# The second weight's blocks begin to be converted in the first stage, and a table of order offsets is set anew

## The chip, the cores and the metric

The kernel runs on one core of one Trainium2 chip. The metric is the device time of one execution in microseconds (us); of the kernel before it is the median of three runs.

## The reference, cut to what matters

Attention over 4 batches and 8 heads with a bias that depends on the two positions, and then a feed-forward pair of matrix products with a gate between them. q, k and v are float32. The two weights of the second half come as 64-bit floats.

```python
# attention: q, k, v are (4, 8, 576, 64)
scores = scale * np.matmul(q, k.transpose(0, 1, 3, 2))
...
x = (psi_rel / psi_i)[..., None]
h = np.maximum(x @ w1 + b1, 0.0)      # 32 hidden values for each pair of positions
scores = scores + (h @ w2).transpose(2, 0, 1)[None]
...
attn_out = softmax(scores) @ v
# second half: x (2304, 512), w_in (512, 2048), w_out (2048, 512)
h = x @ w_in
g = h * (1.0 / (1.0 + np.exp(-h)))
return g @ w_out
```

## The kernel before

The 576 query rows of a head are cut into chunks c = 0 to 3 of 128 rows and c = 4 of 64 rows. The heads go in pairs hp = 0 to 3. The 2304 rows of the second half are five blocks (BLOCKS): two of 384 rows and three of 512.

The program has three stretches. **First**, batches 0 and 1 are done chunk by chunk (ORDER: c = 4, then 0 to 3), and beside them `bias_tile` makes the bias: 36 tiles of 16 rows, each of four relus over a table (kind bias_f, DVE or ACT), a product (bias_mm, PE), an eviction from PSUM in two instructions (bias_ev), a store to DRAM, from which the chunks load it again. **Second**, batches 2 and 3 are done, interleaved with the first two blocks of the second half (`ff_block`). **Third** come the last three blocks (`ff_super`), which trade products for sums.

A chunk (`chunk`) is: scores on PE (s_quad, s_row or s_mm); one DVE pass that adds the bias and takes the maximum (max); exp on ACT; transposes on PE (t_mm); their eviction (p_ev). `visit` ends with the product with v (pv) and stores the result to DRAM (x_d).

`prepare` brings in one block of a weight. `narrow` loads it as 64-bit words (kind ld_wide, 512 KB) into a buffer of pool G and makes float32 of it: one instruction on ACT (abs), four on DVE (clamp, shift, low, sign). `split` then splits it into two halves in another G buffer: split_hi on ACT, split_lo on GpSimd (POOL) or DVE. There are 16 blocks of each weight. A block of w_out stays in its G buffer to the end; G has 27 buffers.

What stands where is set by no loop. Each operation is recorded with the engines that may run it, a duration and a due time; a list scheduler in Python (`Plan.order`) then gives out the operations by due time as engines, buffers and banks come free in its own reckoning. Its answer fixes the instruction order of each engine and of SP, whose queue issues every DMA in that order; a DMA that waits for a buffer holds up those behind it. The due times come from T0, DC, B1, BD and the other constants, and each group of operations has its own offset from the table SHIFT:

```python
group = 4 * self.groups + (0 if "SP" in where else 1 if "PE" in where else 2)
prio += SHIFT.get(group, 0.0)
```

Where PE has nothing to run early on (until WU in the plan's time) the plan puts in `warm_up` products on zeros.

Of the kernel before, what the change touches and what calls it, by code (L numbers as in the profile page):

```python
# [24 lines left out]
FIRST, RAW, QUAD, ORDER = (0, 1), (0, 1), (0, 1, 2, 3), (4, 0, 1, 2, 3)  # L25
# [3 lines left out]
T0, DC, B1, BD, GAP0, DF, DS, WU = 26.19, (3.9, 3.82), 68.9, 4.82, -2.44, 5.0, 12.64, 24  # L29


PACE, LEAD, STEP = (1.32, 2.55), 24.62, (9.49, 8.69)


def f(ap):
# [333 lines left out]
def attention_moe_kernel(ctx: ExitStack, tc: tile.TileContext, q, k, k0, v, small, w_in, w_out, lut, ident_d, out):  # L369
# [668 lines left out]
    def ff_block(blk, t0, step):  # L1038
        xs = split_x(blk, t0 - 8)
        acc = [bank("acc", 1) for _ in range(3)]  # L1040
        for fi in range(NF):
            t = t0 + step * fi
            if blk == 0:
                wr = prepare(t - 5, w_in[fi])
                load("st_in", t - 1, [win_b[fi]], lambda e, wr=wr, fi=fi: SP.dma_start(out=win_d[fi], in_=f(tl(wr).rearrange("p a n -> p (a n)"))), 524288, reads=[wr])
                if wo[fi] is None:
                    wo[fi] = prepare(t - 2, w_out[128 * fi:128 * fi + 128, :])
# [14 lines left out]
    for c in ORDER:  # L1062
        for st in range(8 * c, min(8 * c + 8, 36)):
            bias_tile(st, (t - B1 if c != ORDER[0] else -60) + BD * (st - 8 * c))
        for hp in range(4):
# [3 lines left out]
            for b in FIRST if c == ORDER[-1] else ():  # L1069
                factors(b, hp, sq[b, hp], t)  # L1070
# [96 lines left out]
```

## Time and profile before

| | us |
|---|---|
| median of three runs | 704.21 |
| the runs | 704.07 to 705.24 |
| the profiled execution | 704.64 |
| its span, first to last instruction | 702.8 |
| PE busy in the span | 688.5 |
| VectorE (DVE) busy | 502.9 |
| ScalarE (ACT) busy | 402.1 |
| GpSimd (POOL) busy | 115.2 |

The profiled execution's own time is 1.84 us longer than its span and 0.43 us longer than the median. Busy time is added up over each engine's instructions; PE's records are pipelined, so a product that waits a little for its operands can still count as busy. The granted clock of PE was 0.999 of its higher level (2.4 GHz) over the span.

### The profile page before, as it was taken

How to read it: one execution, taken by the hardware profiler on the slowest of the kernel's cores; microseconds unless marked ns; L12 is line 12 of the kernel's file. 1: busy time of each engine (PE TensorE's matmuls, PEld its weight loads, DVE VectorE, ACT ScalarE, POOL GpSimd, SP SyncE). 2: the span in 40 equal slices, each digit the busy share in tenths (PEclk: the TensorE clock that was granted, in tenths of full speed). 3: DMA queues.
4: the chain of work that ended last, by engine and by line, in shares of the span. 5: the costliest groups of instructions: out<-in, count | busy, mean ns of one | idle time of the engine just before them, and what ended most of it. 6: DMA issues, size and time to landing. Idle time of an engine off the chain costs nothing.

```text
span 702.8 us, 14055 instructions
## 1 busy us (share of the span) xinstructions
PE 688.5 (98%) x5075; PEld 554.0 (79%) x5075; DVE 502.9 (72%) x1127; ACT 402.1 (57%) x882; POOL 115.2 (16%) x134
## 2 busy tenths in 40 slices
PE   9899999999999999999999999999999999999997
PEld 4356677777777777887778888998888888888896
DVE  7889767768988989998986788636374444844433
ACT  8889856667977787877755534423262222433222
POOL 1000000024623231411301111202030010311000
PEclk9999999999999999999999999999999999999999
DMA  8999577678788888658636979676475644795301
GB/s 247 311 325 301 165 258 217 199 219 277 247 248 283 291 257 304 190 204 280 255 127 190 356 270 346 231 271 215 156 237 201 217 157 153 269 280 207 154 1 60
DMA packets 75621, 161.26 MB, mean 229 GB/s; under 512 B 10656, under 2 KB 30752, under 8 KB 75552
## 3 DMA queue, kind: packets, MB, share of 16 engines
q1 hardware_dynamic: 75552, 160.37, 68.8%
q8 instruction: 40, 0.66, 0.4%
q14 instruction: 29, 0.24, 0.1%
HBM read 123.15 MB, written 37.18 MB: 228 GB/s over the span
## 4 chain that ended last, share of the span: by engine, by line
PE 76%; DVE 11%; DMA 5%; ACT 4%; issue 3%; POOL 0%; SPq 0%; DVEq 0%; ACTq 0%; POOLq 0%
PE psum L1001 18%; PE psum L944 15%; PE psum L662 8%; PE psum L785 8%; PE psum L864 7%; PE psum L841 7%; PE psum L753 5%; PE psum L490 3%; PE psum L762 3%; DVE G L769 3%; DMA xp<-x_d 2%; DVE pt L427 1%; DVE w L525 1%; ACT G L497 1%; DVE w L530 1%
## 5 line engine op out<-in xcount | busy, mean ns | idle before, releaser
L1001 PE MATMUL psum<-G 128*128 128x512 f32 x576 | 142.3, 392 | 0.9 <-DVE M L1015 0.5
L776 ACT ACTIVATE G<-G,sm 128x576 f32<-128x576 f32 (+1 forms) x144 | 111.3, 775 | 32.0 <-DVE sm L769 31.5
L1001 PEld LDWEIGHTS psum<-G 128*128 128x128 f32 x576 | 104.1, 188 | 20.2 <-DVE M L1015 1.0
L769 DVE CUSTOM_DVE_ANT_0 G<-psum,G 128x576 f32<-128x576 f32 (+1 forms) x144 | 105.4, 759 | 12.7 <-PE psum L762 5.6
L785 PEld LDWEIGHTS psum<-ident,G 128*128 128x128 f32 x656 | 72.5, 141 | 28.7 <-ACT G L776 12.3
L785 PE MATMUL psum<-ident,G 128*128 128x128 f32 x656 | 92.4, 278 | 2.7 <-DVE th L850 0.5
L662 PE MATMUL psum<-pt,M 128*64 128x128 f32 (+3 forms) x1120 | 85.7, 306 | 0.0
L955 DVE TENSOR_TENSOR M<-psum,M 128x256 f32<-128x256 f32 x72 | 30.2, 422 | 74.7 <-PE psum L944 56.5
L944 PE MATMUL psum<-pt,G 128*128 128x256 f32 x576 | 82.8, 286 | 0.3 <-DVE M L955 0.3
L944 PEld LDWEIGHTS psum<-pt,G 128*128 128x128 f32 x576 | 75.1, 190 | 6.8 <-DVE M L955 4.5
L662 PEld LDWEIGHTS psum<-pt,M 128*64 128x64 f32 x1120 | 61.3, 137 | 21.6 <-issue 4.6
L841 PE MATMUL psum<-M,G 128*128 128x384 f32 x384 | 77.5, 343 | 0.5 <-DVE M L430 0.5
L864 PE MATMUL psum<-G,M 128*128 128x512 f32 x288 | 74.4, 398 | 0.0
L425 ACT ACTIVATE pt<-psum 128x512 f32<-128x512 f32 (+3 forms) x104 | 53.4, 530 | 28.1 <-PE psum L785 20.3
L841 PEld LDWEIGHTS psum<-M,G 128*128 128x128 f32 x384 | 65.5, 188 | 5.0 <-issue 1.5
L982 ACT ACTIVATE M<-M 128x256 f32<-128x256 f32 (+1 forms) x48 | 24.7, 521 | 68.5 <-DVE M L955 67.7
L427 DVE COPY pt<-psum 128x640 f32<-128x640 f32 (+3 forms) x88 | 51.7, 607 | 13.0 <-PE psum L785 10.8
L864 PEld LDWEIGHTS psum<-G,M 128*128 128x128 f32 x288 | 52.0, 189 | 10.8 <-issue 1.8
L425 ACT ACTIVATE M<-psum 128x256 f32<-128x256 f32 x44 | 16.8, 382 | 72.2 <-PE psum L944 71.8
L762 PE MATMUL psum<-G,M 128*128 128x288 f32 x256 | 45.7, 307 | 0.6 <-DVE sm L769 0.6
L430 POOL TENSOR_TENSOR G<-M,G 128x512 fp32r<-128x512 f32 x12 | 15.7, 1313 | 179.7 <-ACT G L425 140.1
L762 PEld LDWEIGHTS psum<-G,M 128*128 128x128 f32 x256 | 37.3, 188 | 6.8 <-DVE sm L769 2.2
(90 smaller groups left out, 962.9 us busy)
## 6 DMA issues: line engine op xcount, KB each, us to landing
G<-ts_d SPq DMA_DIRECT2D x48, 512.0 KB
G<-win_d SPq DMA_DIRECT2D x40, 512.0 KB
G<-bias_d SPq DMA_DIRECT2D x32, 576.0 KB
bias_d<-G SPq DMA_DIRECT2D x36, 295.5 KB
G<-in_w_in_dram SPq DMA_DIRECT2D x16, 512.0 KB
G<-in_w_out_dram SPq DMA_DIRECT2D x16, 512.0 KB
win_d<-G SPq DMA_DIRECT2D x16, 512.0 KB
ts_d<-G SPq DMA_DIRECT2D x16, 512.0 KB
```

Source lines behind the costliest of these rows:

```text
L425: A.activation(out=out, in_=in_, func=AF.Copy)
L427: ENG[e].tensor_copy(out=out, in_=in_)
L662: T.matmul(out=tl(o)[x, d:d + n], lhsT=tl(vs)[:, (s + 1) % 5 * 128 + 64 * a:(s + 1) % 5 * 128 + 64 * a + 64], rhs=tl(pt)[:, s + 5 * a if s ...
L753: T.matmul(out=s[:, hf, 0:288], lhsT=tl(qst)[y, x0 + 128 * a:x0 + 128 * a + 128], rhs=tl(kst)[y, 416 * a:416 * a + 288], start=True, stop= ...
L762: T.matmul(out=s[:, hf, 0:288], lhsT=tl(qs)[:, x0 + 128 * a:x0 + 128 * a + 128], rhs=tl(part)[:, S * a + 288 * hf:S * a + 288 * hf + 288], ...
L769: V.tensor_tensor_reduce(out=mine(p, a).rearrange("p (a n) -> p a n", a=2), in0=tl(sps[a]).rearrange("p (a n) -> p a n", a=2)[:, :, 0:widt ...
L776: A.activation(out=mine(p, a), in_=mine(p, a), func=AF.Exp, scale=-1.0, bias=tl(sm)[:, i + a:i + a + 1], accum_out=tl(sq)[:, 2 * c + a:2 * ...
L785: T.transpose(out=tl(tp)[:, 128 * s:128 * s + 128], in_=tl(p)[:, 128 * (s0 + s):128 * (s0 + s) + 128], identity=ident)
L841: T.matmul(out=tl(hp)[:, 0:TB], lhsT=tl(wr)[:, x, 128 * cc:128 * cc + 128], rhs=tl(xs[cc])[:, y, :], start=(cc + m == 0), stop=(cc == NC - ...
L864: T.matmul(out=tl(acc[i]), lhsT=tl(gg)[:, x, 128 * i:128 * i + 128], rhs=tl(wo[fi])[:, y, :], start=(fi == 0 and m == 0), stop=(fi == NF - ...
L944: T.matmul(out=first(dst), lhsT=tl(w)[:, x, off + 128 * cc:off + 128 * cc + 128], rhs=tl(b)[:, at, y, :], start=(start and cc + i == 0), s ...
L1001: T.matmul(out=tl(acc[i]), lhsT=tl(gg)[:, x, 128 * i:128 * i + 128], rhs=tl(wo[fi])[:, y, :], start=(fi == 0 and j == 0), stop=(fi == NF - ...
```

## The change

A block of w_out is prepared with a due time that is earlier by WL * (1 - fi/16), with WL = 36: by 36 us of the plan's time for the first block and by 2.25 us for the last. The loop over the first stretch is written with PHASES in place of FIRST and ORDER; the phases name the same chunks and the same two batches in the same sequence, and GAP0 is now also added behind the last of them. The constants and all 1,100 or so offsets of SHIFT have new values. The scheduler, the operations, their shapes and their number are as before; only the number of warm-up products on PE differs (35 before, 47 after).

```diff
-FIRST, RAW, QUAD, ORDER = (0, 1), (0, 1), (0, 1, 2, 3), (4, 0, 1, 2, 3)
+RAW, QUAD, WL = (0, 1), (0, 1, 2, 3), 36.0
+PHASES = ((4, (0, 1)), (0, (0, 1)), (1, (0, 1)), (2, (0, 1)), (3, (0, 1)))
...
-T0, DC, B1, BD, GAP0, DF, DS, WU = 26.19, (3.9, 3.82), 68.9, 4.82, -2.44, 5.0, 12.64, 24
+T0, DC, B1, BD, GAP0, DF, DS, WU = 26.13, (3.57, 4.47), 63.81, 5.1, -2.44, 5.0, 11.17, 24
...
-PACE, LEAD, STEP = (1.32, 2.55), 24.62, (9.49, 8.69)
+PACE, LEAD, STEP = (1.32, 4.43), 24.66, (9.49, 9.87)
...
 SHIFT = {
-    0: 4.3, 1: 4.1, 2: 6.1, 4: -7.9, 5: 3.2, 6: 0.6, 8: 3.3, 9: -3.8, 10: -3.8, 12: -6.4, 13: -6.1, 14: -3.2,
...
                 if wo[fi] is None:
-                    wo[fi] = prepare(t - 2, w_out[128 * fi:128 * fi + 128, :])
+                    wo[fi] = prepare(t - 2 - WL * (1 - fi / NF), w_out[128 * fi:128 * fi + 128, :])
...
-    t = T0
-    for c in ORDER:
...
+    t, made, left = T0, set(), {b: 5 for _, some in PHASES for b in some}
+    for c, some in PHASES:
...
-        t += GAP0 if c != ORDER[-1] else 0
+        t += GAP0
```

In the rows that follow, the order before comes first and the order after second. Line numbers after are larger by 2.

**DVE at the start**, up to the first maximum (the custom instruction, shown as ISA, of line 769 before, 771 after). Line 484 (486) is a relu of the bias, line 499 (501) an eviction of a bias tile, which takes two rows.

```order
L499 TENSOR_SCALAR G<-psum,cb 128x31
L499 TENSOR_SCALAR G<-psum,cb 128x560
L484 TENSOR_SCALAR G<-lut_sb,cb 128x512 x3
L484 TENSOR_SCALAR G<-lut_sb,cb 128x496 x4
L484 TENSOR_SCALAR G<-lut_sb,cb 128x480 x2
L484 TENSOR_SCALAR G<-lut_sb,cb 128x448 x4
L484 TENSOR_SCALAR G<-lut_sb,cb 128x464
L769 ISA G,sm<-psum,G 128x640
L769 ISA sm 128x1
```

```order
L486 TENSOR_SCALAR G<-lut_sb,cb 128x448
L501 TENSOR_SCALAR G<-psum,cb 128x79
L501 TENSOR_SCALAR G<-psum,cb 128x512
L486 TENSOR_SCALAR G<-lut_sb,cb 128x480
L486 TENSOR_SCALAR G<-lut_sb,cb 128x448
L486 TENSOR_SCALAR G<-lut_sb,cb 128x480
L486 TENSOR_SCALAR G<-lut_sb,cb 128x432 x3
L486 TENSOR_SCALAR G<-lut_sb,cb 128x464
L501 TENSOR_SCALAR G<-psum,cb 128x111
L501 TENSOR_SCALAR G<-psum,cb 128x480
L771 ISA G,sm<-psum,G 128x640
L771 ISA sm 128x1
```

Two more evictions (of 79 and 512, and of 111 and 480 columns) stand ahead of the first maximum. Counted from the program's start, DVE runs 33 relus and 3 evictions ahead of it before, 34 and 5 after; ACT runs 18 relus and 7 evictions ahead of its first exp before, 22 and 7 after.

**SP's queue late in the first stretch**, where the first weight blocks are loaded (line 508 before, 510 after). in_k is a key of batch 2 or 3, bias_d the bias, in_q a query.

```order
L574 DMA G<-in_k_dram 128x1152
L633 DMA G<-bias_d_103 64x576
L602 DMA M<-in_q_dram 128x256
L508 DMA G<-in_w_in_dram 128x1024
L633 DMA G<-bias_d_103 64x576
L602 DMA M<-in_q_dram 128x256
L508 DMA G<-in_w_out_dram 128x1024
```

```order
L604 DMA M<-in_q_dram 128x256
L510 DMA G<-in_w_out_dram 128x1024
L604 DMA M<-in_q_dram 128x256
L638 DMA G<-bias_d_102 128x2x576
L638 DMA G<-bias_d_100 128x2x576
L604 DMA M<-in_q_dram 128x256
L638 DMA G<-bias_d_101 128x2x576
L680 DMA x_d_136<-xo 128x128
L680 DMA x_d_138<-xo 128x128
L510 DMA G<-in_w_out_dram 128x1024
L604 DMA M<-in_q_dram 128x256
L576 DMA G<-in_k_dram 128x1152
```

Before, the first weight blocks come behind the second key of batch 2; after, three blocks of w_out come ahead of it (the first of them just above the rows shown).

**POOL at the end of the first stretch.** `G<-w,G` is split_lo of a weight, `M<-M` the low half of a query (q_lo), `G<-G 128x576` that of a key (k_lo); line 698 (700) and line 690 (692) are small steps on the sums.

```order
L430 TENSOR_TENSOR G<-G 128x576 x2
L698 TENSOR_SCALAR sq<-sq 128x9
L690 MEMSET sq 128x128 x2
L430 TENSOR_TENSOR M<-M 64x512
L430 TENSOR_TENSOR G<-w,G 128x512
L698 TENSOR_SCALAR sq<-sq 128x9
L690 MEMSET sq 128x128 x2
L430 TENSOR_TENSOR G<-w,G 128x512
```

```order
L432 TENSOR_TENSOR G<-G 128x576 x2
L700 TENSOR_SCALAR sq<-sq 128x9 x2
L432 TENSOR_TENSOR G<-w,G 128x512 x2
L692 MEMSET sq 128x128 x2
L631 MEMSET G 64x64
L632 MEMSET G 64x64
L700 TENSOR_SCALAR sq<-sq 128x9
L692 MEMSET sq 128x128
L432 TENSOR_TENSOR G<-w,G 128x512
L692 MEMSET sq 128x128
L700 TENSOR_SCALAR sq<-sq 128x9
L432 TENSOR_TENSOR M<-M 64x512
```

Three split_lo stand ahead of the first q_lo; before, the first split_lo stood right behind it. Over the program POOL runs 23 split_lo after and 18 before.

## Rows read from the trace of the kernel before

**Rows 1.** The page: span, and busy us (share) xinstructions of two engines.

```profile
span 702.8 us, 14055 instructions
...
PE 688.5 (98%) x5075; PEld 554.0 (79%) x5075; DVE 502.9 (72%) x1127; ACT 402.1 (57%) x882; POOL 115.2 (16%) x134
```

**Rows 2.** Windows: stretch, us, busy of PE, PEld, DVE, ACT, POOL; clock, DMA, GB/s.

```profile
0.00:30.00 30.00, 26.52 (x265) 11.19 (x269) 23.85 (x60) 25.71 (x51) 3.78 (x21) 1.00 0.88 272
30.00:60.00 30.00, 28.74 (x362) 16.34 (x354) 27.73 (x83) 26.45 (x69) 0.00 (x0) 1.00 1.02 331
60.00:150.00 90.00, 89.92 (x952) 66.66 (x952) 67.22 (x160) 62.41 (x141) 3.56 (x6) 1.00 0.71 216
150.00:230.00 80.00, 76.58 (x618) 60.65 (x617) 70.81 (x169) 63.83 (x143) 30.32 (x34) 1.00 0.83 261
230.00:400.00 170.00, 169.20 (x1102) 134.48 (x1102) 148.82 (x321) 119.63 (x254) 39.27 (x36) 1.00 0.71 242
...
450.00:575.00 125.00, 124.35 (x762) 110.12 (x761) 60.35 (x123) 41.47 (x93) 16.19 (x16) 1.00 0.64 214
...
690.00:702.80 12.80, 8.99 (x40) 7.13 (x38) 2.43 (x5) 1.58 (x3) 0.00 (x0) 0.96 0.23 82
```

**Rows 3.** Timeline near the start: start us, us, instruction, [idle before <-releaser].

```profile
8.59 0.96 DVE L499 TENSOR_SCALAR G<-psum,cb 128x543 f32<-128x543 f32 x2
...
20.93 1.25 ACT L482 ACTIVATE G<-lut_sb,cb 128x464 f32<-128x464 f32 x2
...
22.29 0.82 DVE L769 CUSTOM_DVE_ANT_0 G<-psum,G 128x640 f32<-128x640 f32 x1 [1.73 <-ACT G L482]
...
23.22 0.83 ACT L776 ACTIVATE G<-G,sm 128x640 f32<-128x640 f32 x1 [1.05 <-DVE sm L769]
...
23.93 0.77 PE L736 MATMUL psum<-G,M 64*64 64x320 f32 x8 [1.54 <-DVE sm L769]
```

**Rows 4.** The chain of waits of 150 to 270 us: start us, us, what.

```profile
161.55 5.16 DMA M<-in_q_dram
...
167.30 1.28 POOL M L430
...
168.65 1.19 POOL G L430
169.84 6.37 DMA G<-in_k_dram
...
196.36 7.15 DMA xp<-x_d
...
206.70 4.77 DMA xp<-x_d
```

**Rows 5.** Timeline, PE at the end of the first stretch.

```profile
167.89 1.44 PE L753 MATMUL psum<-G,M 64*128 64x288 f32 x8 [1.25 <-DVE sm L769]
```

**Rows 6.** Windows of the instructions on tile w (the conversions): DVE, ACT, POOL.

```profile
150.00:200.00 50.00, 11.05 (x21) 7.70 (x12) 5.14 (x4) 1.00 0.82 261
200.00:250.00 50.00, 23.35 (x42) 10.88 (x17) 4.26 (x3) 1.00 0.83 268
```

**Rows 7.** Timeline: warm-up products ahead of the first scores.

```profile
15.08 0.83 PE L1099 MATMUL psum<-zero 128*128 128x256 bf16 x6
```

**Rows 8.** The chain of waits: products with v, one visit alone and two in a row.

```profile
62.35 2.33 PE psum L662 x40
...
73.35 4.52 PE psum L662 x80
```

**Rows 9.** Tile w by line: duration ns min/median/max, first and last start us.

```profile
L516 DVE TENSOR_SCALAR w<-w x32: 407/420/1447, 162.0 to 343.0; 128x512 f32<-128x512 f32 x32
...
L430 POOL TENSOR_TENSOR G<-w,G x18: 1276/1291/1712, 168.7 to 391.3; 128x512 fp32r<-128x512 f32 x18
```

**Rows 10.** The chain of waits in the third stretch: a load of x for a block.

```profile
476.31 4.88 DMA G<-x_d
```

More of the change, by code (lines that the diff above doesn't have):

```diff
@@ L1060, in attention_moe_kernel @@
     kv, vs, sq = {}, {}, {}
-    t = T0
-    for c in ORDER:
-        for st in range(8 * c, min(8 * c + 8, 36)):
-            bias_tile(st, (t - B1 if c != ORDER[0] else -60) + BD * (st - 8 * c))
-        for hp in range(4):
-            for b in FIRST if c == ORDER[0] else ():
-                kv[b, hp], vs[b, hp], sq[b, hp] = keys(b, hp, t), values(b, hp, t), sums(t)
-            t = visit(hp, [(b, (c,), kv[b, hp], vs[b, hp], sq[b, hp]) for b in FIRST], t)
-            for b in FIRST if c == ORDER[-1] else ():
-                factors(b, hp, sq[b, hp], t)
+    t, made, left = T0, set(), {b: 5 for _, some in PHASES for b in some}
+    for c, some in PHASES:
+        if c not in made:
+            for st in range(8 * c, min(8 * c + 8, 36)):
+                bias_tile(st, (t - B1 if made else -60) + BD * (st - 8 * c))
+        made.add(c)
+        for b in some:
+            left[b] -= 1
+        for hp in range(4):
+            for b in some:
+                if (b, hp) not in kv:
+                    kv[b, hp], vs[b, hp], sq[b, hp] = keys(b, hp, t), values(b, hp, t), sums(t)
+            t = visit(hp, [(b, (c,), kv[b, hp], vs[b, hp], sq[b, hp]) for b in some], t)
+            for b in some:
+                if not left[b]:
+                    factors(b, hp, sq[b, hp], t)
         biases.clear()
-        t += GAP0 if c != ORDER[-1] else 0
+        t += GAP0
     t1 = t + LEAD
     t2 = t1 + NF * STEP[0]
-    rest = [b for b in range(B) if b not in FIRST]
+    rest = [b for b in range(B) if b not in left]
     for hp in range(4):
```

264 rows, old and new, of the table SHIFT are left out of this document.

## The prediction

> **What bounds the kernel now.** I read the page first, for the share of each engine. PE is busy for 688.5 of 702.8 us, DVE for 502.9 [rows 1]. A change of order that leaves PE's products alone can therefore win back at most the 14.3 us in which PE has nothing running, and some of the time in which a product stretches while it waits.
>
> The windows come second, because a share over the whole span hides where those 14.3 us lie. Span less busy gives 3.5 us up to 30 us, 1.3 from 30 to 60, 0.1 from 60 to 150, 3.4 from 150 to 230, 0.8 from 230 to 400, 0.7 from 450 to 575 and 3.8 behind 690 [rows 2]. The last is the tail: the final evictions and stores, which come behind PE's last product whatever the order is. PE ends on out_mm products in a run in both orders (45 before, 60 after), so I leave the tail alone. What is left are two places, the start and the passage from the first stretch to the second, with 4.8 and 3.4 us, and some 2 us in scattered pieces.
>
> The timeline near the start shows what PE waits for there. The first maximum on DVE begins at 22.29 us after 1.73 us in which DVE stood still, the first exp follows after 1.05 us of standing still on ACT, and PE, which needs the bank that the maximum frees, loses 1.54 us [rows 3]. The row names an ACT relu as the releaser, but what a maximum needs besides scores is the bias back from DRAM, so I take the load of the bias for what came last. Around this wait DVE is busy for 23.9 and 27.7 of 30 us, ACT for 25.7 and 26.5 [rows 2]: in the first 60 us both engines are close to full, and standing still there is lost.
>
> The chain of waits shows the passage. A query lands 5.16 us after its load began at 161.55; q_lo on POOL follows at 167.30, then split_lo at 168.65; that frees a buffer of G, and only then does a key's load begin, at 169.84, to land 6.37 us later. Then two loads of x, which the second half needs before its first products, take 7.15 and 4.77 us [rows 4]. PE loses 1.25 us in one piece there [rows 5]. In that window DVE has 70.8 of 80 us to do, and the queues move 261 GB/s [rows 2].
>
> **The change part by part.** Every product and every elementwise operation is still there, so PE's sum stays but for the warm-up products. Six edits have a price.
>
> First, *DVE and ACT ahead of the first maximum*. The order after puts two more evictions and one relu on DVE, and four relus on ACT, ahead of the wait for the bias. An eviction on DVE takes 0.96 us, a relu on ACT 0.63 (half of 1.25) [rows 3]. So 1.92 us and a little go into DVE's 1.73 us of standing still, and 2.5 us into ACT's 1.05. The work is done early rather than added, so at best DVE is 1.7 us further on when the stretch goes on. At worst the first exp comes later by what doesn't fit, 2.5 - 1.05 = 1.5 us, with nothing won, since the first transposes wait for it. Bounds -1.7 and +1.5. I take -0.5: full engines on both sides of the wait speak for the gain, the late exp against it.
>
> Second, *twelve more warm-up products* (35 to 47). Six in a row take 0.83 us, 0.14 each [rows 7]: 1.7 us. They stand ahead of the first transposes, where PE waits for DVE and ACT; it lost 1.54 us in one piece just before them [rows 3]. With that cover they cost nothing, without it 1.7. I take 0.
>
> Third, *the passage*. Three split_lo of w_out stand on POOL ahead of the first q_lo, and no split_lo stands right behind it. In the chain, the key's load waited for that split_lo, hence for the q_lo and the query before it [rows 4]. If the buffer is free when SP comes to the load, the load can start up to 1.2 us earlier (the split_lo's 1.19), or as early as the queue allows. Also the first key of batch 2 stands further forward in SP's queue, ahead of the weights' loads. Against it, three loads of 512 KB stand ahead of the second key, and each takes a buffer of G that stays taken to the end. Bounds: -3.4, all that PE loses there [rows 2], and +1.3, one more wait of the size of the largest [rows 5]. I take -1.2, a third of the loss: the loads of x, 11.9 us in two pieces, stand where they stood, behind the last results of the first stretch, and I count nothing for them.
>
> Fourth, *the conversions spread over the second stretch*. One block costs DVE 23.35 us for 42 instructions, 0.56 each [rows 6], and four or five of them. Before, conversions begin at 162 us [rows 9] and both weights' run at the same pace; after, w_out's begin earlier by up to 36 us and run more thinly behind. What moves out of the second stretch is two or three blocks, 5 to 7 us of DVE, into a window where DVE has 67 of 90 us to do [rows 2], so they are covered where they go. Where they come from PE loses just 0.8 us in 170 [rows 2]. Bounds -0.8 and +1.0 (a POOL or DVE step that comes late for a product). I take -0.4.
>
> Fifth, *fewer changes of the products' kind on PE*. Counted in the order, runs of pv, bias products, float32 scores and everything else follow each other with 165 changes before and 160 after. Two visits' pv in a row take 4.52 us, one alone 2.33 [rows 8]: 0.14 us for a pair of changes. Five fewer: -0.3.
>
> Sixth, *the third stretch*. DS falls from 12.64 to 11.17 and the offsets of its groups rise, so that the due times end up close to what they were; in SP's order some weight loads of the last blocks change places. PE loses 0.7 us in 125 there [rows 2]. Bounds -0.7, and +3: a load that comes late by half of a transfer's 4.88 us [rows 10], once, and a piece more. I take 0.
>
> The sum is -0.5 + 0 - 1.2 - 0.4 - 0.3 + 0 = -2.4 us against the profiled execution: 704.64 - 2.4 = 702.2. That execution lies 0.43 us above the median of the runs, 704.21, so the median after is forecast at **701.8 us**, 0.34% below. A gain of under 0.2%, 1.4 us, can hardly be told from no change on this kernel.
>
> One rule is weighed here. DVE's 512-column conversions take 420 ns in the middle and 1447 at most [rows 9], so something holds one of them up for a full microsecond at times; the POOL split_lo of the same tile takes 1291 ns [rows 9]. The Trainium skill (SBUF — State Buffer, "Who interferes with whom") says that VectorE and GpSimd share one pair of ports under an exclusive lock, and whoever comes second waits for the whole instruction. The trace agrees in size. By that rule POOL's five additional split_lo speak against the change; what they would cost is the third rival.
>
> **The rivals.**
>
> *No change that can be told* (704.2, within 1.4). The waits at the start and in the passage end on transfers: the bias from DRAM, the query, the key, x [rows 3, 4]. The change makes none of these shorter, and the two long loads of x stand where they stood. If the start gains nothing and the passage half a microsecond, the sum is -1.2. For it speaks that PE is already 98% busy.
>
> *Slower by late weights in the third stretch* (706.2). The last three blocks load 72 pieces of 512 KB, each just before its products. Where the new order has such a load closer to its product than a transfer takes, PE stands still for the rest. It decides from about 5 us on, the time of a transfer there (4.88) [rows 10]; two pieces late by 2.2 us each and no gain at the start, 704.2 - 2.4 + 4.4 = 706.2. For it: SP's order differs most there. Against it: PE loses little there before, and DVE and ACT are half idle.
>
> *Slower by POOL against DVE* (705.2). Five more split_lo on POOL hold up DVE for 1.03 us each (1447 - 420 ns) [rows 9], 5 us of DVE; in the passage, where DVE is 89% busy, a third of it reaches PE and the gain of the third edit is lost: 701.8 + 1.7 + 1.2 + 0.5 = 705.2. Against it: as many other POOL instructions go to DVE, and POOL's whole share is 16% [rows 1].
>
> *Slower by the start* (705.9). The first exp comes 1.5 us later, the twelve warm-up products cost their 1.7, and nothing else is won at the start: 701.8 + 0.5 + 1.5 + 1.7 = 705.5, with 0.4 for the bias tiles behind them.
>
> **How the numbers follow.** The forecast and its neighbours on the fast side (down to 698.5, where the start and the passage each give back most of what PE loses) get 0.48. No change gets 0.27. The late weights get 0.12, the start 0.08 and POOL against DVE 0.05: slower 0.25. The range runs from 698.5 to 705.9; below it lies 0.08 and above it 0.11. Alone, the forecast's own range is 700 to 702.8.
>
> **What would show it.** Right: DVE's standing still before the first maximum falls from 1.73 us to under 0.5; PE loses under 2.5 us from 150 to 230 against 3.4; no key's load in the chain begins right behind a split_lo; the third stretch loses as much as before. Wrong: a new wait of PE on a DMA or on DVE behind 440 us, or a first transpose more than 1.5 us later with no less lost up to 60 us. The step that I trust least is the third: it says what the new order frees, and not what it puts in the way.

## The result and the profile after

The change makes the kernel faster: 697.98 us in the median of four runs, against 704.41 for four runs of the kernel before on the same chip. The ratio is 0.9898, interval 0.9873 to 0.9924. One of the four runs took 1152.48 us at a mean granted clock of 0.594 and is left out of the ratio; the median of the other three is 697.2. A second series gave 697.47 (ratio 0.9896, interval 0.9874 to 0.9919). The forecast was 701.8 in a range from 698.5 to 705.9: the sign was right, the gain was 2.7 to 3 times the forecast of 2.4 us, and the time lies below the range. The profiled execution took 696.16 us.

The page of the changed kernel, its span and busy time as in [rows 1]:

```profile
span 694.4 us, 14071 instructions
...
PE 683.2 (98%) x5087; PEld 556.5 (80%) x5087; DVE 500.3 (72%) x1131; ACT 404.1 (58%) x886; POOL 106.3 (15%) x126
```

PE's busy time fell by 5.3 us although it has twelve more products to run. The granted clock is 0.999 in both, so busy time held waits: a product that stands in the pipeline until its operands or its bank come counts as busy. That is the first thing to learn here. The prediction names such waits at its start, but no term of its sum has a price for them.

The windows of the changed kernel, columns as in [rows 2]:

```profile
0.00:30.00 30.00, 27.80 (x265) 12.81 (x266) 24.73 (x61) 26.34 (x52) 3.40 (x21) 1.00 0.88 286
30.00:60.00 30.00, 27.07 (x364) 16.05 (x367) 26.44 (x78) 26.53 (x68) 0.00 (x0) 1.00 0.99 320
...
150.00:230.00 80.00, 79.18 (x647) 63.03 (x646) 74.10 (x174) 68.83 (x151) 30.81 (x39) 1.00 0.86 278
230.00:400.00 170.00, 168.85 (x1101) 137.20 (x1100) 145.12 (x315) 116.72 (x250) 39.14 (x38) 1.00 0.70 241
...
450.00:690.00 240.00, 240.00 (x1470) 215.13 (x1468) 120.10 (x256) 76.67 (x169) 21.09 (x18) 1.00 0.55 186
```

PE stands still for 2.2 + 2.9 = 5.1 us up to 60 (4.7 before), for 0.8 in the passage (3.4 before), for 1.1 from 230 to 400 (0.8 before) and not at all from 450 to 690 (1.5 before, from the next view of the kernel before, same columns):

```profile
450.00:690.00 240.00, 238.50 (x1472) 211.58 (x1471) 121.88 (x247) 80.92 (x178) 32.27 (x31) 1.00 0.57 192
```

Those differences add up to 3.4 us of the 8.4 by which the span is shorter, so standing still shows less than half of the gain. To place the rest I matched the products of the traces by their place in the order and asked when the same amount of PE's work is done. Seven profiled kernels run the first two stretches in the order of before, and seven in the order of after (one of these with six warm-ups fewer); most come from the experiments below, with edits that act later. The table has the median of each seven and its extremes in us, cut at about 27, 123, 166, 232, 336 and 432 us of the kernel before.

| stretch (time before) | order of before | order of after | difference |
|---|---|---|---|
| 0 to 27 | 27.95 (27.2 to 30.8) | 27.87 (26.9 to 28.3) | -0.1 |
| to 123 | 95.54 (95.0 to 96.1) | 95.58 (95.3 to 96.4) | 0.0 |
| to 166 | 42.48 (42.5 to 42.6) | 42.93 (42.9 to 42.9) | +0.45 |
| to 232, the passage | 65.28 (65.1 to 66.7) | 63.21 (62.9 to 65.4) | -2.1 |
| to 336, second stretch | 103.55 (103.5 to 103.6) | 101.79 (101.7 to 101.8) | -1.8 |
| to 432 | 96.31 (96.3 to 96.3) | 96.05 (95.8 to 97.0) | -0.3 |
| to PE's end | 266.8 (before itself) | 263.0 to 263.1 (three kernels) | -3.8 |

The start gave nothing, the passage and the second stretch 3.9 us, and the third stretch, which the prediction put at nothing, gave as much again. The cuts are by the amount of work, which the two orders share out a little differently. At places where both have run exactly the same products (166.6, 237.1, 341.1 and 435.8 us before) the medians say the same: -2.1 for the passage, -1.95 for the second stretch to 341 us, 0.0 from there to 436, and -3.85 behind it in the two kernels themselves. In the passage single executions differ by up to 2.5 us, in the second stretch by 0.1.

The start in the timeline of the changed kernel, columns as in [rows 3]:

```profile
24.04 0.82 DVE L771 CUSTOM_DVE_ANT_0 G<-psum,G 128x640 f32<-128x640 f32 x1 [0.36 <-DMA G<-bias_d]
...
24.97 0.83 ACT L778 ACTIVATE G<-G,sm 128x640 f32<-128x640 f32 x1 [0.25 <-DVE sm L771]
...
26.20 0.76 PE L787 MATMUL psum<-ident,G 128*128 128x128 f32 x5
```

DVE's standing still before the first maximum fell from 1.73 us to 0.36, and the releaser is now named as the load of the bias. But maximum and exp come 1.75 us later than before, and the first transposes 1.58 (26.20 against 24.62).

The passage in the list of what engines wait for, stretch 150 to 230: DVE's waits on transfers (us in total, times, longest) in the kernel before,

```profile
DVE xp L821 <- DMA xp<-x_d: 1.7, 2, 0.9
DVE M L427 <- DMA M<-in_q_dram: 1.4, 1, 1.4
```

and none on DVE in the changed kernel. POOL's wait for a load of x, 10.6 us in one piece before, is gone as well. The chain of waits from 150 to 270 us has two POOL pieces and loads of q, k and x before [rows 4]; in the changed kernel one transfer is left:

```profile
162.47 6.32 DMA G<-in_w_out_dram
```

The third stretch in the chain of waits, 436 to 690 us, shares by line, of the changed kernel:

```profile
by line: PE psum L1003 51.7%; PE psum L946 46.8%; PE psum L866 1.5%
```

It is PE alone. In the kernel before, the chain leaves PE for some 9% of this stretch, for DVE, ACT and the load of x at 476 us among others [rows 10].

### The profile page after: what moved, and what is told of

It is laid out like the page before. It is cut to its first block, busy times and chain, and to the rows that moved or that the text cites. A ratio compares the mean times of both kernels' runs of the same rounds, so it can differ in the third digit from the quotient of the medians.

```text
span 694.4 us, 14071 instructions
## 1 busy us (share of the span) xinstructions
PE 683.2 (98%) x5087; PEld 556.5 (80%) x5087; DVE 500.3 (72%) x1131; ACT 404.1 (58%) x886; POOL 106.3 (15%) x126
## 4 chain that ended last, share of the span: by engine, by line
PE 87%; ACT 4%; DVE 3%; DMA 3%; issue 1%; SPq 1%; ACTq 0%; DVEq 0%
PE psum L1003 19%; PE psum L946 18%; PE psum L787 10%; PE psum L843 9%; PE psum L664 9%; PE psum L866 9%; PE psum L755 4%; PE psum L764 4%; PE psum L492 4%; ACT G L778 2%; DMA G<-in_w_out_dram 1%; DMA G<-win_d 1%; ACT pt L427 1%; PE psum L738 1%; DVE G L771 1%
## 5 line engine op out<-in xcount | busy, mean ns | idle before, releaser
L1003 PE MATMUL psum<-G 128*128 128x512 f32 x576 | 139.6, 391 | 0.0
L787 PEld LDWEIGHTS psum<-ident,G 128*128 128x128 f32 x656 | 72.6, 141 | 29.0 <-ACT G L778 10.6
L427 ACT ACTIVATE pt<-psum 128x640 f32<-128x640 f32 (+3 forms) x110 | 55.9, 527 | 16.2 <-PE psum L787 10.9
L429 DVE COPY pt<-psum 128x640 f32<-128x640 f32 (+3 forms) x82 | 49.3, 612 | 17.5 <-PE psum L787 15.0
L432 POOL TENSOR_TENSOR G<-w,G 128x512 fp32r<-128x512 f32 x23 | 29.7, 1294 | 110.1 <-ACT G L427 102.6
L764 PE MATMUL psum<-G,M 128*128 128x288 f32 x256 | 43.9, 305 | 0.4 <-DVE sm L771 0.4
```

The source lines that it names most:

```text
L427: A.activation(out=out, in_=in_, func=AF.Copy)
L429: ENG[e].tensor_copy(out=out, in_=in_)
L764: T.matmul(out=s[:, hf, 0:288], lhsT=tl(qs)[:, x0 + 128 * a:x0 + 128 * a + 128], rhs=tl(part)[:, S * a + 288 * hf:S * a + 288 * hf + 288], ...
L787: T.transpose(out=tl(tp)[:, 128 * s:128 * s + 128], in_=tl(p)[:, 128 * (s0 + s):128 * (s0 + s) + 128], identity=ident)
L1003: T.matmul(out=tl(acc[i]), lhsT=tl(gg)[:, x, 128 * i:128 * i + 128], rhs=tl(wo[fi])[:, y, :], start=(fi == 0 and j == 0), stop=(fi == NF - ...
```

## The experiments

**The third stretch alone.** Its step DS and its offsets are put into the kernel before, and the old ones into the changed kernel; the block's start is set so that the due times are those of the donor.

```diff
-T0, DC, B1, BD, GAP0, DF, DS, WU = 26.19, (3.9, 3.82), 68.9, 4.82, -2.44, 5.0, 12.64, 24
+T0, DC, B1, BD, GAP0, DF, DS, WU = 26.19, (3.9, 3.82), 68.9, 4.82, -2.44, 5.0, 11.17, 24
...
...   SHIFT from 1460 on: the values of the change
...
-            t1 = max(t1, t + 12)
+            t1 = 499.7 if blk == 2 else t1
```

> The kernel before up to the last three blocks, and those with DS and the offsets of the change: PE's first 606 operations stand as before, its last 333 as after. Theory A (the third stretch gained by its own order, from waits that the profile had inside PE's busy time): the first two stretches as before, the third 3.8 us shorter, 700 to 701. Rival D (the third stretch was shorter because the stretches ahead of it left DVE, POOL and the queues in a better state): 703.5 to 705.

702.4 us beside 705.07, ratio 0.9964 (0.9949 to 0.9978), and theory A holds against D, though with less than its 3.8 us: put into the kernel before, the third stretch's order is worth 2.5 us. Product by product, this trace loses 1.1 us where the halves meet (447 to 483 us of the kernel before) and wins 2.8 behind. The other way round (old DS and offsets in the changed kernel, `t1 = 485.94`):

> The reverse: the changed kernel up to the last three blocks, and those with DS and the offsets of before (PE's last 328 operations stand as before). Theory A: the third stretch gives back its 3.8 us, 700.5 to 702. Rival D: 697 to 698.5.

704.82 beside 705.07, ratio 0.9996 (0.998 to 1.0013): the whole gain is gone, more than theory A's 3.8 us. Not all of that is the third stretch: where the two halves meet, from 436 to 464 us of the kernel before, some 6 us are lost (PE busy 45.47 of 50 us from 400 to 450). Behind that seam its third stretch runs just as before's, within 0.4 us.

**Which part of the third stretch's order?** The kernel before with the new due times for one kind of operation alone; the dictionary THIRD holds the differences for groups of that kind.

```diff
+for _g, _d in THIRD.items():
+    SHIFT[_g] = SHIFT.get(_g, 0.0) + _d
```

Products alone (with 11.17 for DS in out_mm's due time):

> The kernel before with the new due times of the third stretch for the groups of products on PE alone; loads and the elementwise groups keep theirs. Theory Q (the gain of the third stretch is in the order of the products: the pauses of PE at 452, 483, 579 and 599 us, 2.4 us together, are products that stand too close behind the elementwise work that feeds them): 702.0 to 703.3 beside 705.0, as with all due times (0.9964 there), and the pauses gone. Theory R (a stretch's due times are fitted together, and a part of them is worth nothing alone): 704.5 or more. Theory P (POOL holds up DVE there): no change by this, 704.5 to 705.5, as POOL's work stays.

710.82 beside 704.3, ratio 1.0091 (1.0066 to 1.0115). Loads alone:

> The kernel before with the new due times of the third stretch for the loads and stores alone; products and elementwise work keep theirs. Theory S (loads that come too late make the pauses, as the 4.88 us load of x in the chain suggests): 702.0 to 703.3 beside 705.0. Theories Q and P: 704.5 to 705.5, no gain. Theory R: slower than 705, by 1 to 4 us, since loads then come in an order that the products don't follow.

722.24, ratio 1.0244 (1.0221 to 1.0268). Loads and elementwise work without the products:

> The kernel before with the new due times of the third stretch for loads and elementwise work, products keep theirs. Theory Q: no gain, 704.5 to 706. Theory S: 702 to 703.3. Theory R: 704.5 or slower.

708.15, ratio 1.0043 (1.0025 to 1.0062). Neither the order of the products nor that of the loads carries the gain by itself; each part alone costs 4 to 18 us, the loads far more than theory R's 1 to 4. Theories Q and S fall. That says that the parts depend on each other, not what they avoid.

**POOL beside DVE.** The timeline of the kernel before shows what stands ahead of two of PE's pauses in the third stretch, 0.66 us at 452.4 and 1.04 us at 579.2. A pause is counted here as the time from an operation's first product to the next operation's, less what that usually takes.

```profile
451.13 1.48 POOL L430 TENSOR_TENSOR G<-M,G 128x512 fp32r<-128x512 f32 x1
...
451.72 1.44 DVE L986 SCALAR_TENSOR_TENSOR M<-M 128x512 f32<-128x512 f32 x1
...
453.09 0.68 DVE L1015 TENSOR_SCALAR M<-psum 128x512 f32<-128x512 f32 x1
...
453.82 0.50 PE L1001 MATMUL psum<-G 128*128 128x512 f32 x1 [0.50 <-DVE M L1015]
...
578.12 1.49 POOL L887 TENSOR_TENSOR G<-G 128x512 f32<-128x512 f32 x1
...
578.38 1.78 DVE L430 TENSOR_TENSOR G<-M,G 128x512 fp32r<-128x512 f32 x1
...
579.16 0.63 PE L1001 MATMUL psum<-G 128*128 128x512 f32 x2
...
580.22 0.49 PE L1001 MATMUL psum<-G 128*128 128x512 f32 x1 [0.43 <-DVE G L430]
```

At 451.72 a gate (L986) on DVE begins while POOL is at work and takes 1.44 us; the eviction that PE waits for stands behind it. At 578.38 a g_lo on DVE begins while POOL is at work and takes 1.78 us. The out_mm behind it shows 0.43 us of standing still; counted from its first product to the next operation's, it took 1.72 us where its kind takes 0.69. By the Trainium skill (SBUF — State Buffer, "Who interferes with whom") a DVE instruction with two inputs in SBUF and a GpSimd (POOL) instruction that reads SBUF exclude each other, and the second waits for the whole instruction of the first. The rows agree, as the DVE step, which reads two tiles in SBUF, ends 0.55 us after POOL's, near the 0.69 us that it takes undisturbed. The same stretch has a control, DVE steps with one input in PSUM (groups by line of 450 to 690 us: line, engine, operation, tiles and shape with their count, then busy us and mean ns of one, then idle time before them):

```profile
L955 DVE TENSOR_TENSOR M<-psum,M 128x256 f32<-128x256 f32 x68 | 28.5, 422 | 74.0 <-PE psum L944 55.9 <-ACT M L425 17.8
...
L986 DVE SCALAR_TENSOR_TENSOR M<-M,psum 128x256 f32<-128x256 f32 x24 | 10.0, 417 | 1.5 <-ACT M L982 0.6
```

Eleven of the first kind begin while POOL is at work, and the longest of all takes 425 ns. Of the steps with both inputs in SBUF, 19 take over 0.2 us longer than undisturbed, 9.9 us longer together.

The scheduler knows of this: in its reckoning the kinds in its table PORT do not run on DVE and POOL at once. But gate is not in that table, and the g_lo and the x_mul (L887) at 578 us, which are, overlap on the chip all the same.

The test bars POOL from the third stretch of the kernel before:

```diff
+        if group >= 1460:
+            where = {e: t for e, t in where.items() if e != "POOL"}
```

> The kernel before, with no elementwise work of the third stretch on POOL: its 33 instructions there go to DVE, by the planner's choice of engine. Theory P (three of PE's pauses, 0.66 us at 452.4, 1.04 at 579.2 and 0.41 at 599.3, stand behind a DVE instruction of 1.24 to 1.78 us that began while POOL was at work, where the same kind takes 0.6 to 0.75 otherwise): these three go, 702.6 to 703.6 beside 705.0. Theories Q and R: 704.5 to 706, as DVE has 20 us more to do and the products keep their places.

701.44 beside 704.3, ratio 0.995 (0.9931 to 0.9969). The kernel is 2.9 us faster, somewhat more than theory P's three pauses, and P holds. The edit goes through the planner, which also moves about 150 of the 1,600 products of this stretch, most between 615 and 655 us; there the kernel loses 0.4 us. What it wins stands at the pauses: where both kernels have run the same products, it wins 0.8 us from 448 to 454, 1.1 from 576 to 582 and 0.5 from 594 to 603 us of the kernel before, 2.4 of 3.1. The change wins at the same places: 1.0 from 452 to 483, 1.0 from 575 to 585 and 0.5 from 585 to 601 us. From 450 to 690 us the windows of this kernel are

```profile
450.00:690.00 240.00, 239.84 (x1486) 214.27 (x1485) 124.67 (x274) 82.54 (x184) 0.00 (x0) 1.00 0.57 192
```

All that POOL had there, 32.27 us of busy time, went to DVE, and DVE's busy time grew by just 2.8 us, from 121.88. Two forms of DVE show why, in the groups by line of 450 to 690 us, of the kernel before

```profile
L430 DVE TENSOR_TENSOR G<-M,G 128x512 fp32r<-128x512 f32 x34 | 26.2, 798 | 11.6 <-ACT G L425 11.4
...
L986 DVE SCALAR_TENSOR_TENSOR M<-M 128x256 f32<-128x256 f32 x23 | 12.4, 539 | 2.5 <-ACT M L982 2.4
```

and of this one:

```profile
L432 DVE TENSOR_TENSOR G<-M,G 128x512 fp32r<-128x512 f32 x48 | 31.5, 686 | 8.9 <-ACT G L427 8.8
...
L988 DVE SCALAR_TENSOR_TENSOR M<-M 128x256 f32<-128x256 f32 x23 | 9.6, 419 | 1.5 <-ACT M L984 1.5
```

Undisturbed, the two steps take 686 and 419 ns; in the kernel before 798 and 539 in the mean. The changed kernel has 729 and 489: it keeps 22 elementwise instructions on POOL in the third stretch where the kernel before has 33, and they stand elsewhere. With POOL barred no DVE step is held up; in the changed kernel 12 still are, 5.4 us together, but PE never stands still in this stretch.

Then the same bar in the changed kernel:

> The changed kernel, with no elementwise work of the third stretch on POOL: its 22 instructions there go to DVE. Theory P: PE has no pause left there that POOL could make, so little is to be won: 696.3 to 698.0, ratio 0.988 to 0.990, the changed kernel's own. If the gain of POOL's removal in the kernel before (2.9 us) came from something else than its pauses, it should be had again here: 694 to 695. Theory R (an order fitted as a whole loses by any edit): 699.5 or slower.

697.58, ratio 0.99 (0.9882 to 0.9919), the changed kernel's own. The gain is not had twice, and the edit by itself costs nothing, so theory R does not hold for every edit, and the 12 held-up steps that are left cost nothing that these runs can tell. And the reverse, the changed kernel with more of g_lo forced to POOL (41 instructions there in place of 22):

```diff
+        if 1460 <= group and kind == "g_lo" and len(self.ops) % 2:
+            where = {"POOL": where["POOL"]}
```

> The changed kernel, with more of the third stretch's g_lo forced to POOL (31 in place of 11; 41 POOL instructions there in place of 22, and 33 in the kernel before). Theory P: pauses of PE of 0.4 to 1 us come back behind DVE instructions that POOL holds up, and the third stretch gives back 1 to 4 us: 698.5 to 701.5, ratio 0.992 to 0.996. If only where POOL's work stands matters and not how much: 697 to 698, as the changed kernel.

702.81, ratio 0.9979 (0.9968 to 0.9989): 5 us given back, more than expected. Product by product, 6.0 of the 6.7 us by which this trace is longer are lost at one place, 504 to 517 us. Its timeline shows the pause:

```profile
505.00 3.18 POOL L434 TENSOR_TENSOR G<-M,G 128x512 fp32r<-128x512 f32 x2
505.50 1.51 DVE L898 TENSOR_TENSOR G<-G 128x256 f32<-128x256 f32 x1
...
506.94 1.51 DVE L434 TENSOR_TENSOR M<-G,M 128x256 fp32r<-128x256 f32 x1
...
509.84 0.41 DVE L431 COPY M<-psum 128x256 f32<-128x256 f32 x1
...
510.31 1.64 PE L948 MATMUL psum<-pt,G 128*128 128x256 f32 x6 [2.18 <-DVE M L431]
```

Two DVE steps that take 0.42 us elsewhere take 1.51 each beside POOL; the eviction that frees PE's bank stands behind them, and PE waits 2.18 us for it. What the place costs beyond this pause is told at the end. The edit moves some products too, here as there.

Two earlier tries had missed this. The x_lo of the last block alone, taken off POOL in the kernel before (`{"DVE": 0.34} if blk == 4 else ...`):

> The kernel before, with the low halves of the last block's x (x_lo) on DVE alone: 14 on DVE in place of 6 on DVE and 8 on POOL. PE's first 856 operations stand as before, and its last 69. Theory G (the third stretch of before lost its time at the hand-over to the next block, where products wait for an x whose conversion stood late and partly on the slower POOL): 0.8 to 1.5 us less between 575 and 605 us, nothing elsewhere. Rival H (the hand-over waits for the gates of the pair before, whoever converts x): within 0.3 us of before there.

705.58, ratio 1.0007 (0.9992 to 1.0022): no change. POOL's step at 577.91 us, ahead of the same pause, stayed. And eight of them forced to POOL in the changed kernel (`{"POOL": 0.69} if blk == 4 and k % 2 else ...`):

> The reverse: the changed kernel with 8 of the last block's 14 x_lo forced onto POOL (1 stands there in the change). PE's first 879 operations and last 125 stand as in the change. Theory G: 0.8 to 1.5 us more at the last hand-over (570 to 600 us), nothing elsewhere. Rival H: within 0.3 us of the changed kernel.

696.58, ratio 0.9883 (0.9861 to 0.9905), as the change. Theory G, that an x converted late and partly on POOL makes the pause, falls: how much POOL does is not the price, where it stands is.

**The early conversions alone.** The kernel before with the diff's earlier due times for w_out and nothing else, and the changed kernel with WL = 0:

```diff
-                    wo[fi] = prepare(t - 2, w_out[128 * fi:128 * fi + 128, :])
+                    wo[fi] = prepare(t - 2 - 36.0 * (1 - fi / NF), w_out[128 * fi:128 * fi + 128, :])
```

> The kernel before with one edit: the blocks of w_out get their earlier due times (WL = 36), every constant and offset stays as before. PE's order is that of before for its first 175 operations and its last 355. Theory A (each stretch gained by its own new offsets; the early conversions alone do little): the passage from 150 to 230 us changes by less than 1.5 us either way, the third stretch not at all, 703 to 706 in all. Rival B (the early conversions free DVE, POOL and G buffers and so make the gain of the passage and of the second stretch): about 5 us less by 300 us, 699 to 700. Rival C (conversions in the old offsets stand in the way of the keys and queries): over 1 us slower.

709.96 beside 705.07, ratio 1.0081 (1.0064 to 1.0098): in the old offsets the early conversions cost 5 us, as theory C has it in size. That they stand in the way of keys and queries is not shown.

> The changed kernel with WL = 0: all new constants and offsets, the blocks of w_out due when they were before. PE's last 329 operations stand as in the changed kernel. Theory A: close to the changed kernel, 697 to 699.5. Rival B: the passage loses what it gained, 3 to 5 us, 701 to 703.

708.36, ratio 1.0048 (1.0024 to 1.0072), slower than theory A or B had it. Either half alone is slower than both kernels. With WL = 0 most of the loss stands in the passage, in the chain of waits from 150 to 215 us:

```profile
163.27 7.08 DMA G<-in_w_out_dram
...
173.71 6.29 DMA G<-bias_d
...
180.07 3.64 DMA win_d<-G
```

and PE waits 3.0 us in one piece for a maximum there. The third stretch keeps its gain in this kernel.

**Other leads.** The changed kernel with WL at 28 and at 44:

> The changed kernel with WL = 28 in place of 36 (all else as in the change; PE's first 213 operations and last 329 stand as in the changed kernel). The run without the early conversions lost 10 us against the changed kernel. Theory E (what counts is how early the blocks are converted): the loss goes with the distance from 36, so about a quarter, 699.5 to 701. Rival F (the offsets fit WL = 36 alone, and any other value breaks the order in the passage): most of the loss at once, 703 to 708.

> The changed kernel with WL = 44. Theory E: conversions come still earlier, so as the changed kernel or a little better, 696.5 to 698.5. Rival F: as for 28, 701 to 708.

712.95, ratio 1.0116 (1.0094 to 1.0139), and 710.48, ratio 1.0077 (1.006 to 1.0095), where WL = 0 had 1.0048 and WL = 36 has 0.99: no slope in the lead that could be followed, so theory E falls. The offsets fit one value (theory F), and 28 and 44 lose even more than F had it. In both, PE's busy time from 230 to 400 us falls from 168.85 to 162.35 and 163.41 of 170.

**The first stretch alone.** Offsets below 676, T0, DC, B1 and BD of before in the changed kernel, then those of after in the kernel before; the start of what follows is set to the donor's (`t = 162.38`, `t = 173.34`).

> The changed kernel with the first stretch's constants and offsets of before (PE's first 184 operations stand as before, its last 336 as in the change). Theory K (the new first stretch won nothing at the start, and the passage's gain lies in the second stretch's due times and the early conversions): the start as before, the passage still gains at least 2 us, 697.5 to 700. Rival L (the passage gained because the new first stretch leaves DVE and POOL room for the early conversions, so the two belong together): the passage loses 3 us or more, 701 to 706.

> The reverse: the kernel before with the first stretch's constants and offsets of the change (PE's last 540 operations stand as before). The blocks of w_out keep their late due times. Theory K: within 1.5 us of before. Rival L: the room is there but nothing uses it, so no better than before; a loss of over 2 us would say that the first stretch's order costs by itself.

711.66 and 711.73 beside 704.97, both with ratio 1.0098 (1.0077 to 1.0119). The loss lies behind 190 us both times: from 230 to 400 us PE is busy for 162.30 and 165.15 of 170. Theory K falls. Theory L, that the first stretch and the early conversions belong together, agrees with the sign, though both lose more than it had; so does one by which any such splice breaks the fit, and these two runs don't tell them apart.

**The change again, and with six warm-up products fewer** (WU 18 in place of 24):

> The changed kernel once more, unchanged, beside the runs that follow and on their chip: 697 to 699 by either theory. Its profile shows how far two executions of one order differ from stretch to stretch, and so how small a difference between two profiles still means something.

> The changed kernel with WU = 18: 6 warm-up products fewer ahead of the first transposes, and everything else on PE in the same order (its last 949 operations stand as in the change). Theory I (the warm-up products fill a wait and cost nothing): within 0.3 us of the changed kernel from 30 us on. Rival J (they delay the bias products behind them, 0.14 us each): 0.8 us less from 30 us on.

697.47, ratio 0.9896 (0.9874 to 0.9919), and 698.21, ratio 0.9906 (0.9885 to 0.9928): the intervals overlap by most of their width, so six of the warm-ups cost or bring less than these runs can tell. Product by product, the traces with 18 and 24 differ by 0.02 us from 60 to 160 us.

## Why the prediction was right and wrong

The sign was right, in part by luck: half of the gain came where the prediction put nothing.

**First term, the start (-0.5; measured 0.0).** DVE's standing still fell under 0.5 us as forecast, and the first transposes came 1.58 us later with no less lost up to 60 us (5.1 us against 4.7), which the prediction had named as a sign against it. By the table the two cancel. The bounds held.

**Second, the warm-ups (0).** Borne out for six of them.

**Third, the passage (-1.2; measured -2.1, with +0.45 just ahead of it).** The sign and its signs held: PE loses 0.8 us there, under the 2.5 named, and no key's load follows a split_lo in the chain. The size was off; "a third of the loss" counted nothing for the loads of x, and those waits went: DVE no longer comes to a step that needs q or x before they have landed, where it waited 3.1 us for them before.

**Fourth and fifth, the second stretch (-0.4 and -0.3; measured -1.8).** The bound of -0.8 was the time that PE stands still there, and the gain is not in that time: standing still grew by 0.3 us in the windows. It lies in s_mm and out_mm (L762 and L864 of the kernel before). Their products mostly take the same from one start to the next, 0.13 and 0.23 us in the median of both traces; but in the kernel before three s_mm products take 0.30 to 0.51 us and four of out_mm 0.44 to 0.56, 1.85 us more than the median together, and in the changed kernel the longest take 0.29 and 0.33. So the gain is a handful of short waits ahead of the next operation, which count as busy for the most part. What ends them was not tested, and neither was the 0.14 us for a pair of changes of kind [rows 8].

**Sixth, the third stretch (0; measured -3.8).** This is the step that failed: "PE loses 0.7 us in 125 there [rows 2]. Bounds -0.7, and +3". The lower bound took a row on standing still for all that could be won, and a row that covers 125 of 240 us: over the whole of 450 to 690 PE stood still for 1.5. The rest of the lost time stood in PE's busy time, in products that waited in the pipeline. out_mm after out_mm takes 0.68 us in both traces, but counted from operation to operation PE took 5.4 us more than usual before and 1.8 after (usual is the median of the kernel before for the same pair of operations). The main cause is DVE steps held up by POOL ahead of products that need them. Three runs agree on it: POOL barred from the old order wins 2.9 us, most of it at three pauses named beforehand, barred from the new order nothing, and given more work in the new order it costs 5. Some 1.3 us of the 3.8 lie outside these three places, and their cause stays open. The prediction's own sign, "the third stretch loses as much as before", failed.

**The rivals.** "No change" did not come, and neither did the prices of the late weights and of the late exp: no transfer makes PE wait behind 450 us, and the start is even. The time given to the late weights is wrong by its own words: with no gain at the start it is 704.2 - 1.9 + 4.4 = 706.7, not 706.2. In the time of POOL against DVE, the last 0.5 is given no source. POOL against DVE was the right mechanism in the wrong place and with the wrong sign. The prediction counted POOL's additional split_lo (POOL runs them up to 376 us; DVE's longest step of the kind weighed there took 1447 ns before [rows 9] and 1232 after), and did not look where POOL's instructions had stood beside DVE in the third stretch.

What is shown and what is not: that the third stretch's order is worth 2.5 to 4 us and that POOL beside DVE is the main cause is shown by edits. That the passage's gain is the loads that DVE no longer waits for is read from the waits and not isolated, since every edit there broke the fit of the rest. What made the short waits of the second stretch stays open.

## What to carry to other kernels

Do not bound a gain by the bottleneck engine's standing still alone: compare the time from one of its operations to the next with what that pair usually takes, and for the engines that feed it the mean duration of a form with its undisturbed one, and price the excess. Where two engines hold each other up, count the pairs that overlap just ahead of an instruction that the bottleneck waits for, not the load of either engine. And an order fitted to measured times is one piece: of eleven kernels that took parts of one order into the other or moved the lead, ten were slower than the kernel before or no faster.

## What the runs showed of the hardware

A pause of PE was followed by a lower clock. In the changed kernel with more work on POOL, windows around the 2.18 us pause (columns as above; the third from the end is the granted clock):

```profile
505.00:510.00 5.00, 3.13 (x23) 2.77 (x21) 5.00 (x6) 1.64 (x6) 4.04 (x4) 1.00 0.77 259
510.00:512.50 2.50, 1.64 (x6) 1.35 (x6) 1.12 (x4) 1.09 (x3) 0.74 (x1) 0.57 0.00 0
512.50:518.00 5.50, 5.47 (x17) 4.61 (x18) 4.70 (x14) 2.77 (x7) 0.00 (x0) 0.58 0.70 217
518.00:525.00 7.00, 7.00 (x48) 6.46 (x47) 4.15 (x12) 2.34 (x5) 1.29 (x1) 1.00 0.79 282
```

For some 8 us the clock is near the lower of its two levels (1.2 of 2.4 GHz). The place costs 6.0 us in all, where the pause lasts 2.2 and a second one, at 512.53 us, 0.6. The same is seen at the start. In the order of before PE stands still for 1.5 to 2.7 us between 20 and 25 us, and in three of nine such profiles (with 2.30, 2.55 and 2.92 us busy in those five) the clock from 25 to 30 us was 0.66; one with 2.80 us busy kept 1.00. In the order of after PE is busy for all five, and none of seven fell. The medians of the start are equal, but its slow cases, up to 30.8 us in the table, are in the order of before alone.
